# Attention stage: PSUM drained by ScalarE copies, the division moved to GpSimd, and TensorE's groups in a new order

## The chip, the cores and the metric

One NeuronCore of one Trainium2 chip runs the whole program. The metric is the device time of one execution in microseconds (us); lower is better. The engines are TensorE (PE; its weight loads are listed apart as PEld), VectorE (DVE), ScalarE (ACT), GpSimd (POOL) and SyncE (SP, which only starts transfers here).

## The reference, cut to what matters

Three parts follow one another: a linear attention over 4 batches of 576 tokens with 8 heads of 64, a soft mixture of 8 experts with 4 slots each, and a second mixture whose gate is balanced by eight Sinkhorn rounds. The change touches the attention and the slot statistics that run beside it.

```
proj = einsum('bhsd,df->bhsf', x, w_phi)            # for q and for k
proj = proj - max(abs(proj), axis=-1)
phi  = concatenate([exp(proj), exp(-proj)], -1)
kv   = einsum('bhsf,bhsd->bhfd', phi(k), v);  z = sum(phi(k), axis=s)
num  = einsum('bhsf,bhfd->bhsd', phi(q), kv)
den  = einsum('bhsf,bhf->bhs', phi(q), z) + 1e-06
x    = num / den                                     # then logits = x @ phi, softmax over tokens and over slots
```

## The kernel before

The 2304 tokens are 18 tiles of 128 (NT). One loop (line 449) drives the attention: step i works on the keys of tile i and, LAG = 7 steps behind, on the queries of tile t = i - 7. Steps 0 to 6 have keys only, steps 7 to 17 both, steps 18 to 25 queries only. All engines but GpSimd are wrapped in `InOrder` (line 441), so each of them executes in the order in which the code is written; GpSimd is wrapped only at line 527, after the attention.

The work of a step is made of groups; most of what they issue carries the helper's line L51 in the trace, so the tile's name tells the group:

- `project` (line 155; tiles pk, pq): 32 small matmuls into two PSUM banks, then on VectorE for each bank a maximum (mk, mq) and a subtraction (uk, uq), which empties the bank.
- `k_exp` (line 181): four exponentials on ScalarE from uk into phik.
- `kv_acc` (line 189): 64 matmuls of phik with the value tile vt into the accumulator kvacc, one for each batch that the tile touches. Tiles 4 and 13 touch two batches. `kv_finish` (line 208) copies the accumulator to kvs with three ScalarE copies. There is one accumulator buffer, tag "kv".
- `q_transpose` (line 228): 8 transposes of uq into two banks (ut), and behind each bank two ScalarE exponentials into phiq.
- `q_num` (line 255): for each half of the heads 32 matmuls into a bank (num); VectorE adds 1e-6 to the denominator column, takes the reciprocal (rd) and multiplies from PSUM into x.
- `x_turn` (line 281) turns x by 4 transposes (xt or, in the last steps, xl in the accumulator buffer), and ScalarE copies it to xT; `x_logits` (line 293) makes 16 matmuls (lg or xl), and ScalarE copies 32 columns.
- `slot_inputs` (line 306) is a generator. For every group g of four tiles (the last has two) it finds a running maximum (gmt, mx, al), spreads it (dg, gmb), takes exponentials (dd), counts (pcs) and sums x (psi, then si on VectorE); `slot_norm` (line 389) then normalises the logits, with a subtraction and a multiplication on GpSimd (L397, L404) and an exponential on ScalarE between them. The loop advances it by one piece at `si_step`.
- `load_v` (line 139) starts the transfer of a value tile and has GpSimd copy it into vt (L143) and set the ones (L147); vs and vt have two buffers each.

TensorE's order in a full step is: pq(t+1), pk(i+1), xt(t-1), ut(t), lg(t-1), kvacc(i), num(t). PSUM has five 512-column banks A to E beside the accumulator's three; `mm(name, bank)` takes a bank, and a new tile in a bank waits until all readers of the old one are done. In the query-only steps the order is pq(t+1), ut(t), xl(t-1), num(t), lg(t-1), with `halves` (line 223) choosing the banks so that ut and num have banks of their own.

After the last step the generator is run to its end: the last tile's turn and logits, the sums of group 3, the whole of group 4. Between these `keep_busy` (line 377) puts dummy transposes on TensorE. Then psit and sit give the slot inputs, and the first matmul of the expert stage (ph) starts.

The weights of the expert stages are loaded all along, by half units from ScalarE's queue (`load_half`) in steps 7 to 24 and by whole units from SP's (`load_units`); units 5, 6 and 10 wait for the buffers of the query pool (line 508).

Of the kernel before, what the change touches and what calls it, by code (L numbers as in the profile page):

```python
# [7 lines left out]
F32 = mybir.dt.float32  # L8
# [46 lines left out]
def tile_kernel(ctx: ExitStack, tc: tile.TileContext, a):  # L55
# [82 lines left out]

    def load_v(i):
        rows = kp.tile([128, DM], F32, tag="vs", name=f"vs{i}", bufs=2)  # L140
# [4 lines left out]
        parts = parts_of(t)  # L145
        for b1, r0, r1 in parts:
            G.memset(x[r0:r1, :, D:XW], float(b1 == b))  # L147
        vt_t[i] = x
# [6 lines left out]
    def project(pool, nm, x, t):  # L155

        pss, us = [mm(f"p{nm}{t}_{j}", ("AB" if nm == "q" or t < LAG and t % 2 else "CD")[j]) for j in range(2)], []
# [20 lines left out]
    def k_project(t):  # L178
        uk_t[t] = project(kp, "k", kt_t.pop(t), t)

    def k_exp(t):
        us = uk_t.pop(t)
        phik = kp.tile([128, H, 2, F], F32, tag="phik", name=f"phik{t}")
        for j in range(2):
            for c in range(2):
                A.activation(out=phik[:, j::2, c, :], in_=h4(us[j]), func=AF.Exp, scale=1.0 if c == 0 else -1.0)
        phik_t[t] = phik
# [29 lines left out]
    def q_project(t):  # L217
        uq_t[t] = project(qp, "q", qt_t.pop(t), t)

    def alone(i):  # L220
        return i + 1 >= NT

    def halves(t, hh, num=False):
        if t + LAG >= NT:
            return "DC"[hh] if num else "CE"[hh]
        return "EC"[hh] if alone(t + LAG) else "AE"[hh]

    def q_transpose(t, hh):
        ps = mm(f"ut{t}_{hh}", halves(t, hh))
        for j in range(4):  # L230
            PE.transpose(ps[:, j * 128:(j + 1) * 128], uq_t[t][hh][:, j * 128:(j + 1) * 128], ident)
        phiq_t[t, hh] = phiq = [qp.tile([128, 512], F32, tag="phiq", name=f"phiq{t}_{hh}_{c}", bufs=6) for c in range(2)]
        for c in range(2):
            A.activation(out=phiq[c], in_=ps, func=AF.Exp, scale=1.0 if c == 0 else -1.0)
        if hh:
            uq_t.pop(t)
# [7 lines left out]
    pair_t = {}  # L244

    def x_tile(t):
        n = (t + 2) % XR
        if n < 4:
            if n % 2 == 0 or t not in pair_t:
                pair = const.tile([128, 2, DM], F32, tag=f"xx{n // 2}", name=f"xx{t}", bufs=1)  # L250
                pair_t[t - n % 2], pair_t[t - n % 2 + 1] = pair[:, 0], pair[:, 1]
# [3 lines left out]
    def q_num(t, hh):  # L255
        if hh == 0:
            x_t[t] = x_tile(t)
        phiq = phiq_t.pop((t, hh))
        ps = mm(f"num{t}_{hh}", halves(t, hh, True))
        for c in range(2):  # L260
            for j in range(4):
                for g in range(2):
# [6 lines left out]
                    )  # L269
        pv = ps[:, 0:4 * XW].rearrange("p (h w) -> p h w", h=4)  # L270
# [7 lines left out]

    xT_t, xl_t = {}, {}

    def x_turn(t):
        if t + LAG + 1 >= NT:
            xl_t[t] = pacc.tile([128, 1536], F32, tag="kv", name=f"xl{t}")
            ps = xl_t[t][:, 0:512]
        else:
            ps = mm(f"xt{t}", "D" if alone(t + LAG + 1) else "E")
# [6 lines left out]
    def x_logits(t):  # L293
        xT = xT_t.pop(t)
        pl = xl_t.pop(t)[:, 512:1024] if t in xl_t else mm(f"lg{t}", "D" if alone(t + LAG + 1) else "B")
# [10 lines left out]
    def slot_inputs(g):  # L306

        ts, n = groups[g], len(groups[g])
        lgg = lg[:, ts[0]:ts[0] + n, :]
        gm4 = first.tile([128, 4, NS], F32, tag="gd", name=f"gm4{g}", bufs=1)  # L310
        if len(ts) == 2:
# [5 lines left out]
        yield  # L317
        last = g == len(groups) - 1
        pt = mm(f"gmt{g}", "B" if g > 1 else "C")
        keep_busy(last, 5)  # L320
        PE.transpose(pt[:, 0:128], gm4.rearrange("p g j -> p (g j)"), ident)
# [4 lines left out]
        dg = first.tile([NS, NS], F32, tag="gd", name=f"dg{g}", bufs=1)  # L326
        V.tensor_scalar_mul(dg, ident[0:NS, 0:NS], mx[0:NS])
        if g:
            al = first.tile([128, 1], F32, tag="al", name=f"al{g}", bufs=2)
# [3 lines left out]
        yield  # L333
        pm = mm(f"gmb{g}", "B" if g > 1 else "C")
        keep_busy(last, 6)
        PE.matmul(pm[:, 0:NS], ones[0:NS, :], dg, start=True, stop=True)
        dd = first.tile([128, 4, NS], F32, tag="gd", name=f"dd{g}", bufs=1)
        V.tensor_tensor(out=dd[:, 0:n], in0=lgg, in1=pm[:, 0:NS].unsqueeze(1).to_broadcast([128, n, NS]), op=ALU.subtract)
        A.activation(out=dd[:, 0:n], in_=dd[:, 0:n], func=AF.Exp)
        if last:  # L340

            V.tensor_scalar_mul(sels[32 * n:128], sels[32 * n:128], al[32 * n:128])
        yield
        ps, pc = mm(f"psi{g}", "A" if g else "B"), mm(f"pcs{g}", "B" if g else "C")
        keep_busy(last, 4)
        for i in range(n):
            PE.matmul(pc[32 * i:32 * i + 32, 0:2], dd[:, i], ones[:, 0:2], start=True, stop=True)
        for i in range(n):
            PE.matmul(ps[32 * i:32 * i + 32, :], dd[:, i], x_t.pop(ts[i]), start=True, stop=True)
        if g == 3:  # L350
            load_in_x(7)
        r = slice(0, 32 * n)
# [776 lines left out]
```

## Time and profile before

| | |
|---|---|
| median of 3 runs | 1007.1 us (1006.99 to 1008.5) |
| the profiled execution's own time | 1006.96 us |
| its span | 1005.2 us |
| busy share of the span | PE 99%, PEld 93%, DVE 70%, ACT 55%, POOL 57% |
| attention, up to the first ph matmul | 178.55 us from the span's start |
| granted TensorE clock | 1.00 (its upper level) in every stretch |

The span is what the trace covers; the execution's own time has 1.8 us more around it. Busy shares are averages over stages with different limits, and matmul records overlap, so a PE of 99% is not a PE at its peak. What a wait costs is read from the weight loads' idle time (PEld), from the chain of work that ended last and from the times at which groups start.

### The profile page before, as it was taken

To read this page: it belongs to the slowest core of one execution; us is meant where nothing else is said; L and a number is where in the kernel's file an instruction comes from. 1 tells how busy PE (TensorE), PEld (TensorE's weight loads), DVE (VectorE), ACT (ScalarE), POOL (GpSimd) and SP (SyncE) were. 2 spreads that over 40 slices of the span, in tenths; PEclk is the share of its full clock that TensorE was granted. 3 is DMA by queue.
4 is the path that set the end of the run, shared out by engine and by line. 5 is a ranking of instruction groups with operands and counts; after the bars stand their busy time and mean duration, and the time that the engine had idled before them with its cause. 6 is when DMAs were issued, how large, how long until landed. Compare 5 with 4: busy or idle time off the path is not lost.

```text
span 1005.2 us, 27875 instructions
## 1 busy us (share of the span) xinstructions
PE 991.4 (99%) x11638; PEld 936.8 (93%) x11638; DVE 698.9 (70%) x1414; ACT 552.8 (55%) x995; POOL 577.5 (57%) x438
## 2 busy tenths in 40 slices
PE   8999999999999999999999999999999999999998
PEld 7888887459999999999999999999999999999998
DVE  6777876367887676677667676676677667667665
ACT  5665654165666666655565556455555565465452
POOL 2101000135777677858785878578767867777543
PEclk9999999999999999999999999999999999999999
DMA  7766568991003100310031004000400130000111
GB/s 213 220 199 214 167 192 303 392 358 45 1 1 127 43 2 1 126 43 2 2 126 43 2 1 167 3 1 5 165 1 2 35 135 2 1 1 28 59 43 64
DMA packets 25485, 88.84 MB, mean 88 GB/s; under 512 B 3472, under 2 KB 6416, under 8 KB 19600
## 3 DMA queue, kind: packets, MB, share of 16 engines
q1 hardware_dynamic: 19984, 68.05, 19.2%
q10 hardware_dynamic: 5184, 18.88, 6.1%
q8 instruction: 92, 1.51, 0.6%
q14 instruction: 33, 0.27, 0.1%
q0 software_dynamic: 192, 0.13, 0.1%
HBM read 82.33 MB, written 4.72 MB: 87 GB/s over the span
## 4 chain that ended last, share of the span: by engine, by line
PE 96%; DVE 2%; issue 1%; ACT 1%; DVEq 0%; ACTq 0%
PE x L51 39%; PE y L51 20%; PE z L51 16%; PE kvacc L51 3%; PE num L51 3%; PE pq L51 2%; PE ut L51 2%; PE pk L51 2%; PE ps L51 2%; PE po L51 1%; PE ph L51 1%; PE lg L51 1%; PE xt L51 1%; PE xl L51 1%; PE psi L51 0%
## 5 line engine op out<-in xcount | busy, mean ns | idle before, releaser
L51 POOL TENSOR_TENSOR hl_s<-s,hh_s 128x512 fp32r<-128x512 f32 x286 | 365.5, 1300 | 208.2 <-ACT hh_s L51 189.8
L51 PE MATMUL x<-w_t,hh_s 128*128 128x256 f32 x1152 | 204.9, 278 | 0.1
L51 ACT ACTIVATE hh_s<-s 128x512 fp32r<-128x512 f32 x287 | 175.3, 630 | 51.1 <-DVE s L51 48.1
L51 ACT ACTIVATE r<-z 128x512 f32<-128x512 f32 x143 | 85.6, 598 | 166.0 <-PE z L51 164.9
L51 PEld LDWEIGHTS x<-w_t,hh_s 128*128 128x128 f32 x1152 | 173.4, 188 | 1.1 <-ACT xo L51 0.3
L51 DVE SCALAR_TENSOR_TENSOR xo<-x,P,xo 128x256 f32<-128x256 f32 x252 | 120.6, 479 | 70.2 <-PE x L51 70.2
L51 ACT ACTIVATE hh_a<-z 128x512 fp32r<-128x512 f32 x216 | 122.1, 600 | 73.0 <-DVE s L51 71.5
L51 PE MATMUL x<-w_t,hl_s 128*128 128x256 f32 x576 | 159.1, 277 | 0.0
L51 DVE SCALAR_TENSOR_TENSOR s<-z,r 128x512 f32<-128x512 f32 x143 | 98.0, 685 | 87.3 <-ACT hh_a L51 82.7
L51 DVE SCALAR_TENSOR_TENSOR hl_a<-z,hh_a 128x512 fp32r<-128x512 f32 x216 | 146.7, 679 | 2.7 <-ACT hh_a L51 2.7
L51 PEld LDWEIGHTS x<-w_t,hl_s 128*128 128x128 f32 x576 | 108.0, 188 | 0.0
L51 PE MATMUL y<-w_t,hh_s 128*128 128x256 f32 x576 | 103.0, 278 | 0.0
L51 PE MATMUL z<-w_b,hh_a 128*128 128x256 f32 x576 | 102.3, 278 | 0.0
L51 PE MATMUL y<-w_b,hh_s 128*128 128x256 f32 x576 | 101.7, 276 | 0.0
L51 PE MATMUL x<-w_t,hh_a 128*128 128x256 f32 x576 | 101.7, 276 | 0.0
L51 PE MATMUL x<-w_b,hh_a 128*128 128x256 f32 x576 | 101.4, 276 | 0.0
L51 DVE SCALAR_TENSOR_TENSOR s<-z,s 128x512 f32<-128x512 f32 x143 | 97.6, 682 | 3.5 <-POOL hl_s L51 1.4
L51 PEld LDWEIGHTS z<-w_b,hh_a 128*128 128x128 f32 x576 | 86.6, 188 | 2.9 <-issue 2.9
L51 PEld LDWEIGHTS y<-w_t,hh_s 128*128 128x128 f32 x576 | 87.4, 188 | 0.0
L51 PEld LDWEIGHTS y<-w_b,hh_s 128*128 128x128 f32 x576 | 86.8, 188 | 0.0
L51 PEld LDWEIGHTS x<-w_t,hh_a 128*128 128x128 f32 x576 | 86.8, 188 | 0.0
L51 PEld LDWEIGHTS x<-w_b,hh_a 128*128 128x128 f32 x576 | 86.6, 188 | 0.0
(188 smaller groups left out, 1977.1 us busy)
## 6 DMA issues: line engine op xcount, KB each, us to landing
moe_w<-in_moe_w SPq DMA_DIRECT2D x45, 1024.0 KB, 6.6
moe_w<-in_moe_w ACTq DMA_DIRECT2D x36, 512.0 KB, 4.2
vs<-in_vb SPq DMA_DIRECT2D x20, 256.0 KB, 4.1
kt<-in_kT SPq DMA_DIRECT2D x18, 256.0 KB, 3.7
qt<-in_qT SPq DMA_DIRECT2D x18, 256.0 KB, 3.5
out<-xo SPq DMA_DIRECT2D x18, 128.0 KB, 1.7
out<-xo SPq DMA_DIRECT2D x9, 256.0 KB, 2.0
moe_w<-in_moe_w SPq DMA_DIRECT2D x2, 512.0 KB, 10.2
```

The lines of the kernel that those rows point to most:

```text
L51: return lambda *args, **kwargs: self.tc.keep_in_program_order(make(*args, **kwargs))
```

## The change

The numerator no longer leaves PSUM through VectorE: two ScalarE copies per tile put num with its denominators into one SBUF tile, VectorE takes eight reciprocals at once, and GpSimd multiplies, in two instructions (`q_divide`); only the last tile keeps the old way. GpSimd now also runs in program order. `load_v` is split into the transfer and `place_v`, GpSimd's part, one step later. Turning and scoring of x(t-1) now come in the step of num(t), behind it. TensorE's order in a full step becomes num(t), xt(t-1), ut(t+1), pq(t+2), lg(t-1), kvacc(i), pk(i+1). The exponentials of the keys move to the start of their own step, between the copies of num. Each step names its five banks (n0, n1, k0, k1, q1) and rotates them; in the query-only steps they stay. The slot generator becomes plain calls placed by step number (`slot_early`, `slot_late`).

```diff
+    def place_v(i):
         x = kp.tile([128, H, XW], F32, tag="vt", name=f"vt{i}", bufs=2)
-        G.tensor_copy(out=x[:, :, 0:D], in_=rows.rearrange("p (h d) -> p h d", h=H))
+        G.tensor_copy(out=x[:, :, 0:D], in_=vs_t.pop(i).rearrange("p (h d) -> p h d", h=H))
...
-            u = pool.tile([128, 512], F32, tag=f"u{nm}", name=f"u{nm}{t}_{j}", bufs=2 if nm == "k" else 4)
+            u = pool.tile([128, 512], F32, tag=f"u{nm}", name=f"u{nm}{t}_{j}", bufs=2 if nm == "k" else 3)
...
+    def q_transpose(t, hh, bank):
+        ut_t[t, hh] = ps = mm(f"ut{t}_{hh}", bank)
...
+    def q_exp(t, hh):
+        ps = ut_t.pop((t, hh))
+        phiq_t[t, hh] = phiq = [qp.tile([128, 512], F32, tag="phiq", name=f"phiq{t}_{hh}_{c}", bufs=4) for c in range(2)]
         for c in range(2):
             A.activation(out=phiq[c], in_=ps, func=AF.Exp, scale=1.0 if c == 0 else -1.0)
...
-    XR = 7
+    XR = 8
...
+    def q_num(t, hh, bank):
         if hh == 0:
             x_t[t] = x_tile(t)
+            if t + 1 < NT:
+                den_t[t] = qp.tile([128, 2, 4, XW], F32, tag="num", name=f"nums{t}", bufs=1)
...
+        if t + 1 < NT:
+            A.copy(out=den_t[t][:, hh].rearrange("p j w -> p (j w)"), in_=ps[:, 0:4 * XW])
+            return
...
+    def q_divide(t):
+        nums = den_t.pop(t).rearrange("p h j w -> p (h j) w")
+        rd = qp.tile([128, 8, 1], F32, tag="rd8", name=f"rd{t}", bufs=2)
+        V.tensor_scalar_add(rd, nums[:, :, XW - 1:XW], 1e-6)
+        V.reciprocal(out=rd, in_=rd)
+        for hh in range(2):
+            G.tensor_tensor(
+                out=x_t[t].rearrange("p (h d) -> p h d", h=H)[:, hh::2, :],
+                in0=nums[:, 4 * hh:4 * hh + 4, 0:D], in1=rd[:, 4 * hh:4 * hh + 4].to_broadcast([128, 4, D]), op=ALU.mult,
+            )
...
-    PE, V, A, SP = (InOrder(tc, x) for x in (PE, V, A, SP))
+    PE, V, A, SP, G = (InOrder(tc, x) for x in (PE, V, A, SP, G))
...
+    n0, n1, k0, k1, q1 = "CDABE"
+    def slot_early(t, bank):
+        for g in range(LAST):
+            s = t - 4 * g
+            if s == 5:
+                slot_run(g, bank)
+            if s == 6:
+                slot_dd(g, bank)
+            if s == 7:
+                slot_sums(g, bank)
+                if g < 3:
+                    slot_norm(g, 0)
+            if s == 8 and g < 3:
+                slot_norm(g, 1)
+    def slot_late(t, bank):
+        for g in range(LAST):
+            if t - 4 * g == 4:
+                slot_max(g)
+            if t - 4 * g == 6:
+                slot_counts(g, bank)
-    for i in range(NT + LAG + 1):
+    for i in range(NT + LAG):
         t = i - LAG
+        for n in [n for n, (u, _) in enumerate(VBLOCKS) if u == i + 1]:
+            place_v(n)
...
+        if t + 2 < 0:
+            if len(bs) == 1:
+                k_project(i + 1, "CDAB"[(i + 1) % 2 * 2:][:2])
+            kv_acc(i, bs[0])
...
+            continue
+        q_only = i >= NT
+        if 0 <= t:
+            q_num(t, 0, n0)
+        if i in uk_t:
+            k_exp(i, 0, 0)
+        if 0 <= t:
+            q_num(t, 1, n1)
+        if 0 <= t - 1:
+            x_turn(t - 1, None if q_only else n0)
+        if i in uk_t:
+            k_exp(i, 0, 1)
+            k_exp(i, 1, 0)
+            k_exp(i, 1, 1)
...
+        if 0 <= t + 1 < NT:
+            q_transpose(t + 1, 0, n0 if q_only else k0)
+            q_transpose(t + 1, 1, n1)
+        if 0 <= t < NT - 1:
+            q_divide(t)
+        slot_early(t, q1)
+        if 0 <= t + 1 < NT:
+            q_exp(t + 1, 0)
+        if 0 <= t + 2 < NT:
+            q_project(t + 2, (k0, k1) if q_only else (k1, n0))
...
+        if 0 <= t - 1:
+            x_logits(t - 1, q1)
+        if 0 <= t + 1 < NT:
+            q_exp(t + 1, 1)
...
         if bs:
+            late = [(i - 1, b) for b, _, _ in parts_of(i - 1)[1:] if i - 1 >= LAG - 2]
+            for u, b in late + [(i, bs[0])]:
+                kv_acc(u, b)
...
+        slot_late(t, k1 if not q_only else q1)
         if i + 1 < NT:
+            k_project(i + 1, (k0, q1))
+            n0, n1, k0, k1, q1 = k1, n1, k0, q1, n0
+        elif i + 1 == NT:
+            n0, n1, k0, k1, q1 = k0, n1, k1, n0, q1
...
+    qstack.close()
...
+    load_units(wq, 5, 6, 10)
+    x_turn(NT - 1)
+    slot_dd(3, "B")
+    x_logits(NT - 1)
+    slot_max(4)
+    slot_counts(3, "C")
+    slot_sums(3, "A")
+    load_in_x(7)
+    slot_run(4, "B")
+    slot_dd(4, "C")
+    slot_counts(4, "D")
...
+    slot_sums(4, "A", count_all)
```

`slot_max`, `slot_run`, `slot_dd`, `slot_counts` and `slot_sums` are the pieces of `slot_inputs` in their old order and with their old instructions: maximum of the logits; gmt with mx, dg and al; gmb with dd; pcs with cs; psi with si. `slot_norm` is unchanged.

## Rows read from the trace of the kernel before

**Rows 1.** By stretch: length; PE, PEld, DVE, ACT, POOL busy; clock; DMA share, GB/s.
```profile
61.19:69.58 8.39, 8.21 (x221) 7.30 (x222) 6.77 (x15) 4.92 (x10) 0.67 (x2) 1.00 0.55 162
131.64:136.63 4.99, 4.98 (x126) 4.56 (x125) 4.53 (x13) 3.04 (x7) 0.55 (x2) 1.00 0.63 185
...
42.18:122.52 80.34, 78.75 (x2067) 69.03 (x2067) 65.22 (x145) 47.06 (x99) 7.50 (x24) 1.00 0.65 199
...
130.54:168.53 37.99, 36.57 (x844) 32.21 (x842) 29.58 (x84) 20.24 (x46) 2.18 (x6) 1.00 0.67 220
168.53:178.55 10.02, 9.18 (x103) 6.01 (x99) 5.71 (x23) 1.84 (x7) 2.02 (x4) 1.00 1.00 410
```

**Rows 2.** Waits of the weight loads from 36 to 124 us: total, times, longest.
```profile
PEld ut L51 <- PE xt L51: 3.0, 9, 0.3
PEld lg L51 <- DVE uq L51: 1.9, 9, 0.3
```

**Rows 3.** Timeline of the key-only steps: start, length, engine, line, operation.
```profile
14.12 2.21 PE L51 MATMUL kvacc<-vt,phik 128*64 128x65 f32 x64
...
16.25 0.86 PEld L51 LDWEIGHTS pk<-wbd,kt 64*64 64x64 f32 x32
...
16.46 0.61 POOL L143 COPY vt<-vs 128x512 f32<-128x512 f32 x1 [2.20 <-PE kvacc L51]
...
19.30 0.86 PEld L51 LDWEIGHTS pq<-wbd,qt 64*64 64x64 f32 x32
...
20.30 1.15 ACT L51 ACTIVATE phik<-uk 128x512 f32<-128x512 f32 x2 [0.18 <-DVE uk L51]
```

**Rows 4.** Groups by shape, 0 to 179 us: count, busy us, mean ns, idle before.
```profile
L51 ACT ACTIVATE phiq<-ut 128x512 f32<-128x512 f32 x72 | 37.2, 603 | 11.2 <-PE ut L51 10.2
...
L51 DVE TENSOR_TENSOR uq<-pq,mq 128x512 f32<-128x512 f32 x36 | 24.9, 691 | 1.2
...
L51 PEld LDWEIGHTS pk<-wbd,kt 64*64 64x64 f32 x576 | 17.0, 133 | 5.2 <-issue 3.2 <-DMA kt<-in_kT 1.5
...
L51 DVE TENSOR_TENSOR xx<-num,rd 128x256 f32<-128x256 f32 x20 | 8.5, 424 | 1.6 <-PE psi L51 0.9
...
L51 ACT COPY kvs<-kvacc 128x260 f32<-128x260 f32 x4 | 1.6, 395 | 0.0
```

**Rows 5.** Groups by shape on POOL, whole span; same columns.
```profile
L51 POOL TENSOR_TENSOR hl_s<-s,hh_s 128x512 fp32r<-128x512 f32 x286 | 365.5, 1300 | 208.2 <-ACT hh_s L51 189.8 <-DVE s L51 18.2
...
L397 POOL TENSOR_TENSOR lg<-lg,rm 128x128 f32<-128x128 f32 x3 | 1.2, 399 | 32.5 <-DVE rm L51 32.5
```

**Rows 6.** Timeline of one query-only step: start, length, engine, line, operation.
```profile
132.33 1.08 ACT L51 ACTIVATE phiq<-ut 128x512 f32<-128x512 f32 x2 [0.19 <-PE ut L51]
...
133.03 2.10 PE L51 MATMUL num<-kvs,phiq 128*64 128x65 f32 x64
...
134.96 0.62 PE L51 MATMUL xl<-phi,xT 128*64 128x32 f32 x16
...
135.51 1.10 PE L51 MATMUL pq<-wbd,qt 64*64 64x128 f32 x32
...
135.63 0.18 ACT L51 COPY lg<-xl 128x32 f32<-128x32 f32 x1 [0.76 <-PE xl L51]
```

**Rows 7.** Timeline of the slot chain and the end of the attention.
```profile
154.34 0.27 DVE L51 TENSOR_REDUCE rm<-lg 128x4 f32<-128x128 f32 x1
154.76 0.40 POOL L397 TENSOR_TENSOR lg<-lg,rm 128x128 f32<-128x128 f32 x1 [12.59 <-DVE rm L51]
...
170.56 1.04 PE L51 MATMUL psi<-xx,dd 128*32 128x512 f32 x8
...
...
171.70 0.75 DVE L51 SCALAR_TENSOR_TENSOR si<-si,al,psi 128x512 f32<-128x512 f32 x1 [0.63 <-PE psi L51]
...
172.90 0.30 PE L51 MATMUL gmt<-ident,gm 128*128 128x128 f32 x1
...
174.08 0.20 ACT L51 ACTIVATE al<-al 128x1 f32<-128x1 f32 x1 [1.66 <-DVE al L51]
```

More of the change, by code (lines that the diff above doesn't have):

```diff
@@ L153, in load_q, with project @@
         qt_t[t] = x
-    def project(pool, nm, x, t):
-        pss, us = [mm(f"p{nm}{t}_{j}", ("AB" if nm == "q" or t < LAG and t % 2 else "CD")[j]) for j in range(2)], []
+    def project(pool, nm, x, t, banks):
+        pss, us = [mm(f"p{nm}{t}_{j}", banks[j]) for j in range(2)], []
         for p in range(4):
@@ L176, in tile_kernel, with k_project, k_exp @@
     kvacc = {}
[L178 to L187, printed above, removed]
+    def k_project(t, banks):
+        uk_t[t] = project(kp, "k", kt_t.pop(t), t, banks)
+    def k_exp(t, j, c):
+        if (j, c) == (0, 0):
+            phik_t[t] = kp.tile([128, H, 2, F], F32, tag="phik", name=f"phik{t}")
+        A.activation(out=phik_t[t][:, j::2, c, :], in_=h4(uk_t[t][j]), func=AF.Exp, scale=1.0 if c == 0 else -1.0)
+        if (j, c) == (1, 1):
+            uk_t.pop(t)
     def kv_acc(t, b):
@@ L215, in kv_finish, with q_project @@
         kvs_t[b] = kvs.rearrange("p (j h c w) -> p j h c w", j=2, h=4, c=2)
[L217 to L229, printed above, removed]
+    def q_project(t, banks):
+        uq_t[t] = project(qp, "q", qt_t.pop(t), t, banks)
@@ L258, in q_num @@
         phiq = phiq_t.pop((t, hh))
-        ps = mm(f"num{t}_{hh}", halves(t, hh, True))
+        ps = mm(f"num{t}_{hh}", bank)
         for c in range(2):
@@ L285, in x_turn @@
         else:
-            ps = mm(f"xt{t}", "D" if alone(t + LAG + 1) else "E")
+            ps = mm(f"xt{t}", bank)
         for kc in range(KC):
@@ L343, in slot_inputs, with slot_dd @@
-        yield
-        ps, pc = mm(f"psi{g}", "A" if g else "B"), mm(f"pcs{g}", "B" if g else "C")
-        keep_busy(last, 4)
-        for i in range(n):
-            PE.matmul(pc[32 * i:32 * i + 32, 0:2], dd[:, i], ones[:, 0:2], start=True, stop=True)
+    def slot_dd(g, bank):
+        n = len(groups[g])
+        pm = mm(f"gmb{g}", bank)
+        keep_busy(g == LAST, 6)
+        PE.matmul(pm[:, 0:NS], ones[0:NS, :], run["dg"], start=True, stop=True)
+        dd_t[g] = dd = first.tile([128, 4, NS], F32, tag="gd", name=f"dd{g}", bufs=1)
+        V.tensor_tensor(out=dd[:, 0:n], in0=lgs(g), in1=pm[:, 0:NS].unsqueeze(1).to_broadcast([128, n, NS]), op=ALU.subtract)
+        A.activation(out=dd[:, 0:n], in_=dd[:, 0:n], func=AF.Exp)
+        if g == LAST:
+            V.tensor_scalar_mul(sels[32 * n:128], sels[32 * n:128], al_t[g][32 * n:128])
@@ new lines, in slot_counts, with slot_sums @@
+    def slot_counts(g, bank):
+        n = len(groups[g])
+        r = slice(0, 32 * n)
+        pc = mm(f"pcs{g}", bank)
+        keep_busy(g == LAST, 4)
+        for i in range(n):
+            PE.matmul(pc[32 * i:32 * i + 32, 0:2], dd_t[g][:, i], ones[:, 0:2], start=True, stop=True)
+        if g == 0:
+            V.tensor_copy(out=cs[r], in_=pc[r, 0:2])
+        else:
+            V.scalar_tensor_tensor(out=cs[r], in0=cs[r], scalar=al_t[g][r], in1=pc[r, 0:2], op0=ALU.mult, op1=ALU.add)
+    def slot_sums(g, bank, between=None):
+        ts, n = groups[g], len(groups[g])
+        r = slice(0, 32 * n)
+        dd = dd_t.pop(g)
+        ps = mm(f"psi{g}", bank)
@@ L454, in tile_kernel @@
             load_v(n)
[L455 removed]
+        for u in {2: [0], 4: [1], 5: [2]}.get(i, [t + 4] if 2 < t + 4 < NT else []):
             load_q(u)
```

187 lines of the change are left out of this document (65 added, 122 removed).

## The prediction, made before the change was run

> **What bounds the kernel now.** I read the page first: TensorE is busy through the span and keeps its upper clock, and the change ends where the expert stage begins, so only the attention's end can move. The stretches come next [rows 1]. A full step takes 8.39 us with 7.30 us of weight loads, a good query-only step 4.99 us. VectorE (6.77), ScalarE (4.92) and GpSimd (0.67) are below TensorE in a full step: TensorE sets the pace, and an engine relieved gains only what TensorE now waits for. The waits of the weight loads name that [rows 2]: in nine steps ut waits behind the turn of x, 0.3 us each, and lg for the bank that VectorE empties, 0.2 us each. Then the timelines of a key-only step, a query-only step and the end [rows 3, 6, 7].
>
> **The sum**, against the profiled execution's 1006.96 us, which lies 0.1 us under the median of 1007.1 us. Points in time are those of the trace; the expert stage's first matmul is at 178.55.
>
> Start (steps 0 to 7): more waits. Each projection keeps VectorE for four operations of some 0.69 us [rows 4], then come two pairs of exponentials of 1.15 us [rows 3]. Before, pk waits 3.2 us there [rows 4]. After, kv of tile 4 stands first in its step (pq(0) no longer covers it) and waits for exponentials that end at 21.45, 1.1 us after it could go on; pq(0) waits 0.65 us for pk(5)'s bank, ut(0) 1.5 us for pk(6)'s, pq(1) 0.5 us. These four are my count from the code with the durations just named; they make 3.75 us, so +0.5. By 42.18 [rows 1] the new order has also one pq and one ut more behind it, 1.9 us, so its step 8 starts at 44.6.
>
> Full steps: a gain. Nothing in the new order is asked for just when it is ready: the bank of x's turn comes free with the copy of num's first half 0.5 us ahead, lg has a pq between it and xT, pk finds its banks drained a group earlier. So a full step is the plain work of a query-only step (4.99) and of a key-only one, 19.30 - 16.25 = 3.05 [rows 1, 3]: 8.04. By weight loads, 4.56 and 2.81 of them against 7.30 seen in a step, it would be 7.97. I take 8.0; the ends are 8.39 (no gain) and 7.8. Nine such steps are 72.0 us. Step 17 has no pk: 7.0. The second batch of tile 13 is 1.9, psi 0.9 (the sum of group 1 has moved on to step 18), and the small groups of two slot chains 1.9, at 0.3 to 0.4 us each (gmt has 0.30 [rows 7]). Together 83.7 us.
>
> One wait in step 14, **the queue on GpSimd**. `place_v` for tile 15 needs the value buffer of tile 13's second batch, whose kv now runs in step 14 itself, behind lg. GpSimd is in order: its copy starts 0.13 us after that kv (before, 14.12 + 2.21 to 16.46) and takes 0.61 [rows 3]; behind it stand the two multiplies of `q_divide`, then the subtraction of `slot_norm`, 0.40 [rows 5], and ScalarE, in order too, has this norm's exponential ahead of those of ut. pk(15) wants ut's bank. A multiply of 128x256 has no row: 0.40 us for 128 columns and 1.30 for 512 [rows 5] bound it, and on the line between it is 0.69, which I take. From kv's end 0.13 + 0.61 + 1.38 + 0.4 + 0.3 + 1.08 of exponentials [rows 6], with some 0.15 of hand-overs, is 4.0; the other kv, 2.0, fills half of it. So 2.0 us of wait (1.4 to 3.2 with the bounds).
>
> VectorE's multiply from PSUM takes 0.424 us [rows 4]. The Trainium skill's GPSIMD Engine Reference (Performance versus the Vector engine) says that GpSimd is the wrong place for elementwise arithmetic with two inputs, measured there at 1.96 times VectorE. By that it would be 0.83 us, an estimate, and the wait 0.3 us longer.
>
> So step 18 starts at 44.6 + 83.7 + 2.0 = 130.3. In rows 1 its counterpart is 130.54.
>
> Query-only steps: **two banks for four tiles**. In these steps num's first half, ut's first half and the next num share n0, the second halves n1. num's second half must wait for both exponentials of ut's second bank, and ScalarE has the copy of lg ahead of them, which waits for lg, TensorE's last group of the step. The chain from lg's end: 0.05 to the copy, some 0.07 until the next can start, 1.08 for two exponentials, 0.1 back to TensorE: 1.3 [rows 6]. In its shadow lies num's first half, half of 134.96 - 133.03, so 0.93 after its start. Each step waits 0.37: 5.35 instead of 4.98. Where a slot piece puts something before the first exponentials, more. psi to si 1.14, si 0.75 [rows 7], rm and the way to GpSimd 0.42 and the subtraction 0.40 [rows 7], the norm's exponential and 1.08: some 4.1 us from ut's end, under which TensorE has psi, pq (1.10) and lg (0.55) [rows 6], 2.5 in all; that is a wait of 1.6, and 0.3 more at the second half. This hits steps 18 and 22 (t = 11, 15). At t = 13 the exponential al comes 1.18 us after gmt [rows 7] and costs 0.7. From step 18's start to the end of num(17): 9.6 (both nums), 5.35, 6.0, 5.6, 7.7 and 4.25 (no pq): 38.5. So num(17) ends at 168.8; before, at 168.53 [rows 1].
>
> End: the new order has turn and logits of tile 16 behind num(17), and one accumulator buffer, so the last turn waits for lg(16)'s copy instead of x(17): turn of 16, copy, lg and copy make 2.2 us behind num(17), the division of x(17) 1.4 (my estimates from the durations above). psi of group 3 (1.04 [rows 7]) now stands between the last logits and gmt instead of under the copy of xT. +0.8 and +1.0, -0.1 for shorter VectorE queues: 11.7 instead of 10.02 [rows 1].
>
> The sum: 168.8 + 11.7 = 180.5, which is 1.95 after 178.55. 1006.96 + 1.95 gives **1008.9 us**, 1.8 over the median.
>
> Costed at nothing: the 34 copies of num on ScalarE (0.395 us for this shape [rows 4]) and the multiplies elsewhere. A full step's ScalarE then has 4.92 + 0.8 of 8.0 us, and x is wanted a whole step later. Uncovered, the copies would cost 0.4 a half. VectorE loses two multiplies a tile, 0.85 us [rows 4], which gives nothing by itself. The loads of units 5, 6 and 10 still follow num(17); DMA is full from there, with a share of 1.00 [rows 1], and as ph comes later behind num(17) their cover grows. SP's value loads wait for `place_v` but are two steps early.
>
> **Rivals.**
> - Faster: the exponentials of ut are not held up by the norm. If the subtraction gets through GpSimd and VectorE before lg ends, step 14 loses its 2.0 and steps 18 and 22 lose 1.5 each: 1008.9 - 5.0 = 1003.9, and the gain of the full steps, 9 x 0.39 = 3.5, shows. For it: GpSimd starts its subtraction 0.42 us after rm does [rows 7], so the norm itself is short. Against: rm stands behind si, and si behind psi, on an in-order queue. It decides where the norm's exponential ends less than 1.3 us after ut.
> - Slower: ScalarE is the bound of the tail. If its operations don't overlap (exponentials 0.6 each, the copy of lg 0.2 whole), the chain of each query-only step grows by 0.15 for every operation in it, the steps to 5.45, those with slot pieces by 0.4 more, together 2.0: 1010.9. For it: one exponential is 0.603 [rows 4], so the 1.08 for two [rows 6] rests on an overlap. Against: ScalarE has 3.04 of 4.99 us there. It decides from the point where ScalarE is still at work when num's first half ends.
> - The full step does not shrink: ut or lg finds another wait of the size of rows 2, and 3.5 us are not gained: 1012.4.
>
> **How the numbers follow.** A measurement of this kernel tells about 0.2%, 2 us, from no change. The forecast lies just under that. My case has 0.42, the faster rival 0.28, the two slower ones 0.22 and 0.08. My own case spreads by the bounds of the multiply (-0.6 to +1.2) and of the full step (-1.8 to +3.5), so a third of it lies beyond +2. That gives faster 0.26, same 0.36, slower 0.38. The range for 8 in 10 reaches from just under the faster rival, 1003.5, to between the slower ones, 1011.5; the likeliest case alone has 1007 to 1010.5.
>
> **What would show it.** Full steps of 8.0 us with no wait of ut and lg; one hole of 2 us before pk in step 14, released by ScalarE, with GpSimd's copy of vt in the middle of the step; query-only steps of 5.3 to 5.4 us where num waits for ScalarE's phiq; two holes near 1.6 us behind psi; 11.7 us from num(17) to ph. Query-only steps of 5.0 us, or no hole in step 14, would make it wrong on the fast side; full steps of 8.4 us on the slow side.

## The result, and the profile after

The change makes the kernel slower: 1015.45 us (1011.89 to 1016.9, five runs) against 1007.1 us (1006.8 to 1008.5, five runs), a ratio of 1.0073 (95%: 1.0051 to 1.0094). A second series of the same two kernels (e5 below) gave 1014.2 against 1007.86 us, 1.0066 (1.0053 to 1.0078). Forecast were 1008.9 us and a range of 1003.5 to 1011.5. The profiled execution took 1015.84 us with a span of 1014.1, 8.9 more than before.

The forecast had given points in time, so the miss can be located:

| point | forecast | after | added to the miss |
|---|---|---|---|
| num of step 8 starts | 44.6 | 46.22 | 1.6 |
| num of step 18 starts | 130.3 | 134.92 | 3.0 |
| num of the last block ends | 168.8 | 174.03 | 0.6 |
| ph, the expert stage, starts | 180.5 | 186.46 | 0.7 |
| from there to the end | 826.7 | 827.6 | 1.0 |

The busy times by stretch in the kernel after (same columns as [rows 1]); in this order a full step, step 8, step 14, step 20 of the query-only ones, all of those, and the end:

```profile
65.04:73.07 8.03, 8.03 (x222) 7.38 (x224) 5.36 (x10) 5.45 (x12) 1.85 (x4) 1.00 0.62 194
46.22:56.55 10.33, 8.29 (x224) 7.50 (x220) 5.72 (x10) 6.48 (x15) 1.84 (x4) 1.00 0.63 199
98.50:111.26 12.76, 11.03 (x294) 9.47 (x293) 5.91 (x11) 5.75 (x13) 2.76 (x7) 1.00 0.48 154
147.42:153.92 6.50, 5.51 (x134) 4.85 (x130) 5.03 (x13) 3.63 (x11) 1.47 (x3) 1.00 0.63 200
134.92:174.03 39.11, 35.37 (x812) 30.33 (x805) 22.42 (x55) 22.61 (x55) 9.19 (x18) 1.00 0.63 197
174.03:186.46 12.43, 9.97 (x103) 6.60 (x103) 5.88 (x24) 2.51 (x8) 2.31 (x5) 1.00 1.00 403
```

A full step takes 8.03 us instead of 8.39 [rows 1] and TensorE is busy in all of it: the gain is there. VectorE falls from 6.77 to 5.36 us a step, ScalarE rises from 4.92 to 5.45 and GpSimd from 0.67 to 1.85. Step 8 has TensorE idle for 2.0 of 10.33 us, step 14 for 1.7 of 12.76, the query-only steps for 3.7 of 39.11.

The waits of the weight loads from 36 to 135 us (total, times, longest); those of ut for xt [rows 2] are gone, those of lg for VectorE are down from nine to two of 0.2 us (eight more of up to 0.2 us stand under "issue"; the matmuls in front cover them, since TensorE is busy in all of a full step), and two long ones have come:

```profile
PEld num L51 <- issue: 3.9, 11, 2.2
PEld pk L51 <- ACT phiq L51: 1.9, 1, 1.9
```

The second is the wait forecast for step 14. Its timeline is as forecast, with GpSimd's copy in the middle:

```profile
106.64 0.61 POOL L51 COPY vt<-vs 128x512 f32<-128x512 f32 x1 [8.21 <-PE kvacc L51]
107.25 1.19 POOL L51 TENSOR_TENSOR xx<-nums,rd 128x256 f32<-128x256 f32 x2
108.39 0.40 POOL L51 TENSOR_TENSOR lg<-lg,rm 128x128 f32<-128x128 f32 x1
108.83 0.31 ACT L51 ACTIVATE lg<-lg 128x128 f32<-128x128 f32 x1 [5.41 <-POOL lg L51]
109.05 1.06 ACT L51 ACTIVATE phiq<-ut 128x512 f32<-128x512 f32 x2
110.16 1.17 PE L51 MATMUL pk<-wbd,kt 64*64 64x128 f32 x32 [1.73 <-ACT phiq L51]
```

The first was not forecast. Step 8's timeline shows TensorE stopping inside one group, after 54 of the 64 matmuls of num; the profile names no releaser, and from 49.2 us on VectorE, ScalarE and GpSimd are idle too:

```profile
46.22 1.85 PE L51 MATMUL num<-kvs,phiq 128*64 128x65 f32 x54
50.10 0.51 PE L51 MATMUL num<-kvs,phiq 128*64 128x65 f32 x10 [2.04 <-issue]
```

One row of the DMA queues, from 47.50 to 47.75 us (packets, MB, share of 16 engines), led to a theory. A block of 16 KB of instructions begins to arrive there, at 47.56; the block before had begun at 39.85, while in undisturbed steps they come 4 to 5 us apart:

```profile
q8 instruction: 1, 0.02, 24.6%
```

ScalarE's queue had started two halves of expert weights, 512 KB each, shortly before. In the kernel before, the same two halves started 2.8 us apart, at 37.85 and 40.69; in the new order they start 0.65 us apart. The next half, that of step 8, starts only behind the hole, so the 1 MB of step 7 alone can bear on it. The DMA engines were 84 to 93% busy from 42 to 46 us. In the timeline of after:

```profile
42.01 0.38 ACTq L51 DMA_DIRECT2D moe_w<-in_moe_w  x1
42.66 0.34 ACTq L51 DMA_DIRECT2D moe_w<-in_moe_w  x1
51.25 0.33 ACTq L51 DMA_DIRECT2D moe_w<-in_moe_w  x1
```

TensorE, then, may have had no instructions left. The Trainium skill (Runtime: NRT & Kernel Launch, Instruction fetch mechanics) says that an engine's instructions are streamed in 16 KiB blocks by a DMA queue of its sequencer, at a cost that is mostly hidden. The size agrees with this row; whether the cost is hidden is what the runs ask.

### The profile page after: what moved, and what is told of

It reads as the page before. It is cut to its first block, busy times and chain, and to the rows that moved or that the text cites. A ratio compares the mean times of both kernels' runs of the same rounds, so it can differ in the third digit from the quotient of the medians.

```text
span 1014.1 us, 27882 instructions
## 1 busy us (share of the span) xinstructions
PE 992.6 (98%) x11638; PEld 939.3 (93%) x11638; DVE 682.1 (67%) x1344; ACT 563.0 (56%) x1029; POOL 597.2 (59%) x472
## 4 chain that ended last, share of the span: by engine, by line
PE 94%; DMA 2%; ACT 1%; DVE 1%; issue 1%; POOL 0%; ACTq 0%; DVEq 0%
PE x L51 39%; PE y L51 19%; PE z L51 16%; PE num L51 4%; PE kvacc L51 3%; PE pk L51 2%; DMA moe_w<-in_moe_w 2%; PE pq L51 2%; PE ps L51 1%; PE po L51 1%; PE ut L51 1%; PE ph L51 1%; PE xl L51 1%; PE lg L51 1%; PE xt L51 1%
```

## The experiments

All runs in one table. Times in us of the profiled execution; "query-only" is from num of step 18 to num of the last block, "end" from that num's end to ph. Each ratio is against runs of the kernel before in the same series; their medians were 1007.1 us for after, 1009.17 for e1 to e4, 1007.86 for e5 to e8 and 1010.01 for e9 to e11.

| run | num of step 8 | step 8 | step 14 | query-only | end | ph | ratio to before (95%) |
|---|---|---|---|---|---|---|---|
| after | 46.22 | 10.33 | 12.76 | 36.89 | 12.4 | 186.46 | 1.0073 (1.0051 to 1.0094) |
| e5, after again | 46.29 | 9.45 | 12.76 | 36.89 | 12.4 | 184.72 | 1.0066 (1.0053 to 1.0078) |
| e1, norm late | 45.54 | 9.23 | 10.89 | 36.23 | 12.4 | 182.09 | 1.0017 (0.9998 to 1.0036) |
| e2, three vt | 46.24 | 9.24 | 10.89 | 36.87 | 12.4 | 183.05 | 1.0036 (1.0019 to 1.0054) |
| e3, weights later | 46.17 | 8.03 | 12.75 | 36.88 | 12.4 | 184.80 | 1.0051 (1.0035 to 1.0068) |
| e4, VectorE divides | 47.78 | 9.86 | 13.51 | 39.01 | 13.7 | 205.28 | 1.0250 (1.0220 to 1.0281) |
| e6, scores first | 46.01 | 9.77 | 10.89 | 32.02 | 12.4 | 179.06 | 1.0002 (0.9992 to 1.0012) |
| e7, end regrouped | 47.64 | 14.44 | 12.76 | 36.90 | 11.3 | 190.06 | 1.0076 (1.0060 to 1.0091) |
| e8, all mended | 45.50 | 8.03 | 10.89 | 32.02 | 12.9 | 178.44 | 0.9985 (0.9969 to 1.0001) |
| e9, turns back | 45.39 | 8.02 | 10.89 | 32.02 | 11.3 | 176.49 | 0.9958 (0.9944 to 0.9972) |
| e10, start banks | 43.90 | 8.03 | 10.89 | 32.01 | 10.7 | 175.16 | 0.9960 (0.9945 to 0.9976) |
| e11, weights back | 44.04 | 10.48 | 10.89 | 32.02 | 10.7 | 175.74 | 0.9977 (0.9963 to 0.9992) |

The expert stage behind ph is the same program in all of them and took 825.6 to 830.7 us in these executions, so ph is the sharper measure of an edit, the ratio that of the kernel.

**The norm in step 14 (e1, e2).** e1 moves its first half behind the step's kv; e2 gives vt a third buffer:

```
# e1, in slot_early: taken out; in slot_late: put in
+            if t - 4 * g == 7 and g < 3:
+                slot_norm(g, 0)
# e2
-        x = kp.tile([128, H, XW], F32, tag="vt", name=f"vt{i}", bufs=2)
+        x = kp.tile([128, H, XW], F32, tag="vt", name=f"vt{i}", bufs=3)
```

> The first half of the slot norm (VectorE's maxima, GpSimd's subtraction, ScalarE's exponential) is moved from the middle of its step to behind the step's accumulation of keys and values; nothing else moves. Theory A (the norm's exponential stands in ScalarE's queue ahead of the exponentials of ut and waits there for a GpSimd that is itself held, by the copy of vt in step 14 and by its multiplies in steps 18 and 22): step 14, from the start of num to the start of the next num, falls from 12.76 us to 8.0 to 8.5, steps 18 and 22 fall from 7.40 and 7.64 to about 6.0 each; 4.4 + 1.4 + 1.6 = 7.4 us less than the changed kernel, about 1008. Rival B (what is late in these steps is GpSimd's result x or the copy of vt itself, and TensorE would only wait one group later, in the turn of x or in the accumulation of the next step): the three steps and the one after each lose less than 1.5 us together, and the time stays above 1013.5.

> The placed values get three buffers instead of two, so that GpSimd's copy in step 14 need not wait until the late accumulation of step 13's block has read its buffer; the norm stays where it is. Theory A (GpSimd's queue is held by that copy): the copy runs some 8 us earlier, the multiplies wait for the copies of num alone, and step 14 falls from 12.76 us to between 8.0 and 9.2; steps 18 and 22 stay at 7.4 and 7.6, since there is no copy of vt in them; 3.6 to 4.7 us less than the changed kernel, about 1011. Rival B (the two multiplies of 0.6 us and the norm's subtraction hold ScalarE whatever the copy does, as in steps 18 and 22): step 14 keeps a wait of 1.3 us or more and stands at 9.5 or above, 3 us less at the most. Rival E (the wait is not of GpSimd at all): 12.8 as before.

Step 14 went from 12.76 to 10.89 in both, and the wait of pk is gone from both. The 8.0 to 8.5 and 8.0 to 9.2 written down were a slip: the forecast itself has the second batch of tile 13 and psi in this step, some 2.9 us more than a full step. The wait was 1.87 us, and either half of its cause removed is enough: in e2 the norm still stands ahead of the exponentials, but its exponential starts 6.0 us after the step's num instead of 10.3, with GpSimd's multiplies long done, and pk waits for nothing:

```profile
102.97 0.31 ACT L51 ACTIVATE lg<-lg 128x128 f32<-128x128 f32 x1 [1.08 <-POOL lg L51]
106.82 1.10 PE L51 MATMUL pk<-wbd,kt 64*64 64x128 f32 x32
```

In the query-only steps rival B was right about e1: step 18 fell from 7.40 to 6.00 us, but step 19 rose from 5.1 to 6.23. The norm's exponential then stood ahead of the next step's copies of num, and ut waited for those:

```profile
140.26 0.31 ACT L51 ACTIVATE lg<-lg 128x128 f32<-128x128 f32 x1 [1.67 <-POOL lg L51]
140.74 0.38 ACT L51 COPY nums<-num 128x260 f32<-128x260 f32 x1
140.89 0.88 PE L51 MATMUL ut<-ident,uq 128*128 128x128 f32 x6 [0.50 <-ACT nums L51]
```

**The hole in step 8 (e3, e5, e11).** e3 moves the loads of two weight units out of steps 7 and 8 into steps 16 and 17 (the first halves are shown; the second ones move in the same way):

```
-    attn_units = {7 + n: (wa, n) for n in range(4)}
+    attn_units = {7 + n: (wa, n) for n in range(2, 4)}
+    twice = {16: (wa, 0), 17: (wa, 1)}
...
+        if i in twice:
+            load_half(*twice[i], 0)
```

> The expert weights that ScalarE's queue fetches in steps 7 and 8 (two units, 2 MB) are fetched in steps 16 and 17 instead; the instructions and their order on TensorE, VectorE and GpSimd are the same. In the changed kernel TensorE stands 2.04 us in the middle of num in step 8 with no operand missing, and the fetch of a block of instructions that begins at 47.5 us, as the weights' packets end, comes 2.4 to 2.6 us before it goes on. Theory C (TensorE has run out of instructions, whose fetch came late behind the weights' packets): with no weights in steps 7 and 8 the next block's fetch begins 4 to 5 us after the one before it and not 7.75 us, the hole is gone or under 0.4 us, step 8 takes 8.0 to 8.5 instead of 10.33, and the time is about 2 us less than the changed kernel's, 1013.5, unless a hole opens in steps 16 and 17. Rival D (the hole belongs to the place in the program, or to a wait that the profile does not name): it stays between the same instructions with 1.5 us or more, and the time is within 0.7 us.

> The changed kernel once more, on the same chip as the three below. Theory C (TensorE now and then runs out of instructions, whose blocks are fetched late behind other transfers, so the hole varies from execution to execution): the hole inside num of step 8 has another length than 2.04 us (the two kernels with the same program up to there showed 0.94 us, at the same instruction), other steps show holes of up to 0.6 us that the first profile did not have, and the time is 4 to 9 us above the kernel before on the same chip. Rival D (a fixed wait of the program): 2.04 us again, within 0.1.

In e3 num runs through, and the block that had come at 47.56 us came at 44.11. The timeline of e3:

```profile
46.17 2.09 PE L51 MATMUL num<-kvs,phiq 128*64 128x65 f32 x64
48.19 0.66 PE L51 MATMUL xt<-ident,x 128*128 128x128 f32 x4
```

Step 8 took 8.03 us. Smaller holes opened elsewhere (0.49 us in step 9, 0.52 us where the weights had gone), so that ph came 1.7 us earlier and not 2.3. In e5, the same kernel as the one forecast, the hole was 0.94 us, before the same ten records, so it is no fixed wait; the new holes in other steps that theory C had also expected of e5 did not come. e11 is e10 with the weights back in steps 7 and 8:

> The same kernel as the start_banks run, but with the weights of two units fetched in steps 7 and 8 again, as in the changed kernel. Theory C (the fetch of TensorE's instructions is late behind the weights' packets): step 8 shows a hole of 0.9 to 3.7 us again, inside num, where the kernel without these weights has none, and the time is 0.5 to 2 us more. Rival D: no hole of more than 0.4 us, the same time within 0.5 us.

The hole came back, in e11's timeline:

```profile
48.07 0.51 PE L51 MATMUL num<-kvs,phiq 128*64 128x65 f32 x10 [2.19 <-issue]
```

ph came only 0.6 us later than in e10, which has holes of 0.45, 0.69 and 0.46 us in steps 9, 13 and 17 instead.

Over all profiles: in the seven with weights in steps 7 and 8 and the new order on TensorE (after, e1, e2, e5, e6, e7, e11) the block came 5.8 to 10.1 us after the one before, and the hole was 2.04, 0.94, 0.94, 0.94, 1.47, 3.69 and 2.19 us, always before the same ten records. TensorE went on 1.2 to 1.6 us after the block's packet had ended, whether the packet came late or took long (in e5 it came early and took 2.2 us, in the others 1.0). In the four without (e3, e8, e9, e10) the block came 4.3 to 4.6 us after the one before, with no hole in step 8. In e4 the block came 7.2 us after the one before, but TensorE, slower there, needed it only 1.9 us after its packet's end. That it is the weights, by their times those of step 7, is shown; whether two halves 2.8 us apart, as before, would have left a hole was not run.

That TensorE lacks instructions can be read from the traces, though no row names a releaser. Number TensorE's records from 0 in the order of their start, semaphore instructions included. The gap of step 8 stands before record 2241 = 193 + 8 x 256 in all seven profiles. In the thirteen traces TensorE has 27 gaps of 0.2 us or more inside a group for which no releaser is named, and all of them stand before a record whose number is 193 plus a multiple of 256. The queue q8 brings 92 blocks to TensorE's 23,575 records in after, which is one for every 256 records; and record 193 + 256 m never starts sooner than 1.19 us after the end of the queue's m-th packet, in any of the thirteen traces. So TensorE stands until its next block is there, and a late block shows as a gap if TensorE gets to the border first. The weights are only one cause of a late block: the holes of steps 9, 13 and 17 lie at such borders too. The Trainium skill's "mostly hidden" holds at most of these borders, and does not hold at these 27.

**Is the division needed for the order? (e4)** The new order with the division of before on VectorE:

```
-        if 0 <= t < NT - 1:
-            q_divide(t)
...
-        if t + 1 < NT:
-            A.copy(out=den_t[t][:, hh].rearrange("p j w -> p (j w)"), in_=ps[:, 0:4 * XW])
+        if False:
+            A.copy(out=den_t[t][:, hh].rearrange("p j w -> p (j w)"), in_=ps[:, 0:4 * XW])
```

> The new order of the groups with the division of before: num is read from PSUM by VectorE (sum, reciprocal, multiply for each half), the ScalarE copies and the GpSimd multiplies are left out. Theory F (the new order needs num's bank free at once, since the turn of x writes it two groups later): VectorE comes to the first half only behind the four operations on the keys' projection, 2.8 us after the step's start, and needs 0.8 us more, so that the turn of x starts at 3.6 instead of 2.2 us; full steps take 9.2 to 9.7 instead of 8.0, and ten of them make 12 to 15 us more, less some 3 us of the wait in step 14, for which GpSimd no longer has multiplies ahead of the norm: 1021 to 1028. Rival G (VectorE has room, being busy 5.6 to 7.2 of 8.0 us in a step, and the order alone brings the shorter step): full steps of 8.0 to 8.4, and the time is within 3 us of the changed kernel or below it.

Theory F, and worse than it expected: full steps of 9.85 us, ph 18.8 us later, and 1035.9 us in all instead of 1021 to 1028, though VectorE is busy only 6.69 us of a step. The row to read is xt's wait for VectorE, which reaches num only behind the keys' four operations:

```profile
70.39 0.15 DVE L51 TENSOR_SCALAR rd<-num 128x4 f32<-128x4 f32 x1
71.36 0.63 PE L51 MATMUL xt<-ident,x 128*128 128x128 f32 x4 [1.78 <-DVE rd L51]
```

So with VectorE's operations in this order the new order on TensorE needs the copies on ScalarE to run at 8.03 us. Two things were not run: an order in which VectorE takes num ahead of the keys' operations, and the new division in the old order.

**The query-only steps (e6).** ScalarE's exponentials of ut come first, lg's matmuls and copy behind them, and the norm's subtraction runs on VectorE, ahead of the sums:

```
-        slot_early(t, q1)
         if 0 <= t + 1 < NT:
             q_exp(t + 1, 0)
+        slot_early(t, q1)
...
-        if 0 <= t - 1:
+        if 0 <= t - 1 and not q_only:
             x_logits(t - 1, q1)
         if 0 <= t + 1 < NT:
             q_exp(t + 1, 1)
+        if 0 <= t - 1 and q_only:
+            x_logits(t - 1, q1)
...
+                if g < 3:
+                    slot_norm(g, 0)
                 slot_sums(g, bank)
-                if g < 3:
-                    slot_norm(g, 0)
...
-            W.tensor_tensor(out=cc, in0=cc, in1=rm.to_broadcast([128, n, NS]), op=ALU.subtract)
+            V.tensor_tensor(out=cc, in0=cc, in1=rm.to_broadcast([128, n, NS]), op=ALU.subtract)
```

> On ScalarE the exponentials of ut go ahead of what can wait: the first half's ahead of the slot operations, in the query-only steps the second half's ahead of the copy of lg; the norm's subtraction runs on VectorE instead of GpSimd, ahead of the sums of the slots. Theory A (in steps 14, 18 and 22 the exponentials wait for a norm held by GpSimd; in the other query-only steps they lose 0.3 us to the copy of lg, and 0.7 us in step 21 to the running maximum's exponential): step 14 falls from 12.76 to 10.9, and the six query-only steps from 36.9 us to 32.5 to 34 in all; 4.8 to 6.3 us less at the point where the experts' stage begins. Rival H (these steps are bound by the sum of TensorE's and ScalarE's work, and what is taken out of the way of the exponentials comes back as a wait for num's copies or for lg, as when the norm was moved to the step's end: 36.2 instead of 36.9): query-only steps 36 or more.

Theory A: 36.89 became 32.02 us, a little more than expected. By step: 18 lost 1.40, 20 lost 1.39 (the expectation calls it 21; the exponential al stands ahead there), 22 lost 1.65, and the other three 0.13 to 0.15 each. Three steps of e6 (19, 20, 22) show TensorE without a gap, so nothing more is to be had there from ScalarE. What each of these edits is worth alone was not run. The stretches of the three steps:

```profile
138.48:143.46 4.98, 4.98 (x131) 4.57 (x128) 3.97 (x10) 3.18 (x8) 1.54 (x3) 1.00 0.70 234
143.46:148.54 5.08, 5.08 (x131) 4.67 (x129) 4.17 (x12) 3.03 (x9) 1.48 (x3) 1.00 0.62 209
154.14:160.13 5.99, 5.99 (x141) 4.74 (x134) 4.51 (x11) 3.62 (x9) 1.23 (x2) 1.00 0.59 185
```

**The end (e7, e8, e9).** In the kernel after, one short wait follows another behind the last num:

```profile
175.35 0.66 PE L51 MATMUL xl<-phi,xT 128*64 128x32 f32 x16 [0.62 <-ACT xT L51]
176.29 0.66 PE L51 MATMUL xl<-ident,x 128*128 128x128 f32 x4 [0.29 <-ACT lg L51]
177.68 0.66 PE L51 MATMUL xl<-phi,xT 128*64 128x32 f32 x16 [0.40 <-ACT xT L51]
179.56 0.29 DVE L51 TENSOR_TENSOR gm<-lg 128x128 f32<-128x128 f32 x1 [1.95 <-PE psi L51]
```

e7 turns the last x into a bank of its own and reorders what follows:

```
+        if t == NT - 1:
+            x_turn(t, "C")
         if 0 <= t - 1:
             x_logits(t - 1, q1)
...
-    x_turn(NT - 1)
     slot_dd(3, "B")
-    x_logits(NT - 1)
-    slot_max(4)
+    x_logits(NT - 1, "E")
     slot_counts(3, "C")
+    slot_max(4)
+    slot_run(4, "B")
     slot_sums(3, "A")
...
-        keep_busy(g == LAST, 5)
```

> Only the order behind num of the last step differs: the last x is turned into a bank of its own instead of waiting for the copy of lg of the x before it, lg of the last x follows at once, the maximum of the last two blocks goes to TensorE ahead of the sums of the four before (its tiles have buffers of their own, so that it need not wait until those sums are read), and five turns that only fill TensorE's time are left out. Theory I (the end is 2.4 us longer than before because these waits follow one another: 0.62, 0.29 and 0.40 us for xT and lg, 1.0 us of VectorE for the sums, 0.6 us of filling): from the end of num of the last block to the experts' stage 10.0 to 10.6 us instead of 12.4. Rival J (the end is one chain of short operations of VectorE and ScalarE, which these waits only fill): 11.7 or more.

The end took 11.3 us: 1.1 gained, half of what theory I expects and more than J allows. Its total was lost elsewhere, by a longer hole and by the granted clock (PEclk, the last but two of the columns). The clock was at its lower level from 34.6 to 38.0 us, behind the wait of 1.62 us before ut, which left it at 1.00 in nine other profiles; num of step 8 started 1.4 us later for it, at 47.64. Then the hole of step 8 was 3.69 us long in this execution, and the clock fell again, so that step 8 took 14.44 us, 6.4 more than 8.03:

```profile
34.59:38.00 3.41, 3.36 (x54) 3.04 (x56) 1.09 (x3) 3.08 (x6) 0.00 (x0) 0.50 0.27 76
53.00:58.00 5.00, 4.82 (x46) 4.36 (x49) 0.38 (x2) 3.30 (x7) 1.19 (x2) 0.50 0.35 109
```

e8 has the edits of e2, e3, e6 and e7 together, and pq(0) back in step 4:

> The changed kernel with all of it: the queries' first projection back in step 4, three buffers for the placed values, the weights of steps 7 and 8 fetched in steps 16 and 17, the exponentials of ut first and the norm's subtraction on VectorE, the end regrouped. If the theories hold, the experts' stage begins 1.5 (start) + 1 to 2 (the hole of step 8) + 1.9 (step 14) + 3 (query-only steps) + 2 (end) = 9.4 to 10.4 us earlier than at 186.46 us, at 176 to 177 us against 178.55 in the kernel before, and the time is 1.5 to 2.5 us under the kernel before on the same chip. Rival (the holes open at other places, or the start is bound by VectorE's two projections whatever their order): 179 us or later, and the time is within 2 us above the kernel before.

The time is 2.0 us under the kernel before, as expected, but the interval of the ratio reaches 1.0001. ph, at 178.44, lies between theory and rival. It misses 176 to 177: the start gave 0.7 instead of 1.5, small holes opened in steps 9, 13, 15 and 17, and the end grew to 12.9 us. In this end the clock fell, and psi took 1.94 us instead of 1.04 [rows 7]; the stretch and the row in e8's timeline:

```profile
169.70:173.40 3.70, 3.62 (x16) 1.50 (x16) 1.49 (x5) 0.20 (x1) 0.00 (x0) 0.54 1.00 379
```

```profile
170.10 1.94 PE L51 MATMUL psi<-xx,dd 128*32 128x512 f32 x8
```

e7's profile shows the same end without the turns at a clock of 1.00, so the fall does not follow from the order of the end alone. e9 is e8 with the five turns back in slot_run:

```
+        keep_busy(g == LAST, 5)
         PE.transpose(pt[:, 0:128], gm_t.pop(g).rearrange("p g j -> p (g j)"), ident)
```

> The kernel with everything mended, with the five turns put back that only fill TensorE's time while VectorE takes the maximum of the last two blocks. In the kernel without them the granted clock was 0.54 of the upper level from 169.7 to 173.4 us, and the sums of the slots took 1.94 us instead of 1.04, the next six filling turns 1.49 instead of 0.88. Theory K (that idleness let the clock fall to the lower level): the turns, 0.77 us, stand in a wait of 0.70 us, the clock stays at 1.00, the sums take 1.04 us again, and the experts' stage begins 1.2 to 1.6 us earlier than without them, seen from the end of num of the last block (12.8 us there): 11.2 to 11.6. Rival L (the clock falls there anyway, for what came before): 12.8 to 13.5.

Theory K: psi took 1.06 us, the end 11.3, and the kernel is faster than before, by 0.4%. It does not rest on one profile: the mean clock of an execution was under 1.00 in ten of e8's eleven and in one of e9's nine. The timeline of e9:

```profile
168.70 0.77 PE L51 MATMUL busy<-ident 128*128 128x128 f32 x5
169.64 1.06 PE L51 MATMUL psi<-xx,dd 128*32 128x512 f32 x8
```

**The start (e10).** On top of e8:

```
-            k_project(i + 1, (k0, q1))
+            k_project(i + 1, (q1, k0) if t == -2 else (k0, q1))
...
-            q_transpose(t + 1, 0, n0 if q_only else k0)
+            q_transpose(t + 1, 0, n0 if q_only else q1 if t == -1 else k0)
...
-    slot_run(4, "B")
-    slot_sums(3, "A")
+    slot_sums(3, "A", lambda: slot_run(4, "B"))
```

> The kernel with everything mended, with two further edits. First, the keys' projection of step 6 is written into banks E and A instead of A and E, and the first half of the first ut into C instead of A, so that it need not wait until VectorE has read the keys' projection there (a wait of 1.62 us at 32.6 us that the profile calls issue). Theory M (that wait is the bank): ut follows the projection within 0.1 us, and num of step 8 starts 0.8 to 1.3 us earlier, at 44.2 to 44.7 us. Rival N (VectorE's queue, with three projections of 2.77 us in a row, is the bound of steps 5 to 7): ut is early, but what follows waits, and step 8 starts within 0.3 us of 45.5. Second, at the end the maximum of the last two blocks goes behind the sums of the slots on TensorE and no turns only fill the time there: with the clock kept, the end takes 10.6 to 11.2 us from the last num instead of 12.8. Both: the experts' stage begins at 175.2 to 176.5 us and the time is 2.5 to 4 us under the kernel before.

Theory M, and more than the 0.8 to 1.3 us it expected: num of step 8 starts 1.6 us earlier than in e8. What the profile of after calls "issue" was a bank still to be read by VectorE: ut starts 0.1 us after the subtraction that reads the bank ends, and this gap stands before a group and at no border of a block. First the rows of after, then that of e10:

```profile
32.44 0.69 DVE L51 TENSOR_TENSOR uk<-pk,mk 128x512 f32<-128x512 f32 x1
33.23 1.06 PE L51 MATMUL ut<-ident,uq 128*128 128x128 f32 x8 [1.62 <-issue]
```

```profile
30.44 1.09 PE L51 MATMUL ut<-ident,uq 128*128 128x128 f32 x8
```

Step 8 starts at 43.90, and ph comes at 175.16, 3.4 us before that of the kernel before. The time, 0.9960, is not under e9's: the expert stage took 830.1 us in e10's profile and 826.1 in e9's. Some 0.8 us of the difference come up 24 to 56 us behind ph, where po waits for VectorE's hz in e10 (0.72 us) and not in e9, and 3.0 us between 125 and 260 us, where one matmul of x takes 281 ns on average instead of 277, at a granted clock of 1.00 in both. Why stays open. e10's end, 10.7 us as expected, has no filling turns, and its clock was 1.00 in all six executions: the turns matter in e8's order, not in every one.

## Why the prediction was wrong

- **Full steps, 8.0 us**: right, 8.03; TensorE is busy in all of such a step, as its row in the table by stretch shows.
- **"Together 83.7 us" for steps 8 to 17**: the step that failed. It took these steps to be the plain work of their groups and nothing else, and so put at nothing that TensorE can stand still for want of instructions. With step 14's wait it was 85.7 us; 88.70 were measured. The late blocks cost 2.3 us in step 8 (by step length, against 8.03), 0.4 in step 9 and 0.8 in step 13; without them it would have been 85.2. How much it is differs between executions: in e5's the same steps took 86.9 us, 1.2 over the forecast, and there the start, 1.7 us, is the largest part of the miss. The sign was to be had. In the kernel before, too, a pk stops after eight records, at a border of a block; this wait is part of the 3.2 us that [rows 4] give for pk, which the forecast took for waits for VectorE:

```profile
36.34 0.89 PE L51 MATMUL pk<-wbd,kt 64*64 64x128 f32 x24 [1.23 <-issue]
```

- **The wait in step 14**: right in mechanism and size, 1.87 us against 2.0. The multiply of 128x256 took 0.61 us (mean of 34), against 0.69 from the line (0.70 by its own two ends). By the Trainium skill's GPSIMD Engine Reference (Performance versus the Vector engine) it would have been 0.83, an estimate; next to VectorE's 0.424 [rows 4] the 0.61 is 1.4 times, not the 1.96 measured there for 2048 elements.
- **Query-only steps**: right in kind, 39.1 against 38.5 us, but the sum is nearer than its terms, which is partly luck. By what e6 took away, the norm's waits cost 1.40 and 1.65 (forecast 1.6 + 0.3 each); al cost 1.39, not 0.7; the bank chain 0.15 a step, not 0.37 (half of 134.96 - 133.03 is 0.97, so its own rows give 0.33).
- **Start, "step 8 starts at 44.6"**: mis-sized by 1.6 us. The bank waits were there as counted (ut(0) 1.62 for 1.5), but the exponentials that kv of tile 4 waits for ended at 22.30 instead of 21.45, 0.85 late: 0.3 from the first loads on, the rest from a hole in pk(4), which took 1.77 us instead of 1.10. The hole lies at a border of a block, the term that steps 8 to 17 lack too; in e5 there is none, and all of the delay, 0.9 us, is there before pk(4). The pq of step 6 took 1.37 us instead of 1.1, in e1 to e6 too, so that is no late block; some 0.4 us more have no name here. e10 shows that 1.6 us of such a start lie in two choices of banks.
- **End, 11.7**: 12.4. The sequence was right. The 0.7 us more lie somewhere in the chain of short operations and the filling turns; no run tells which, and e7 and e10 show only that 1.1 and 1.7 us can be had there by another order.
- **The rest of the span** was taken as unchanged; it took 1.0 us more, within what it varies by.
- **Rivals**: the faster one needed the norm off the exponentials' way. It did not happen, but e6 makes it happen: step 14 and the query-only steps give 1.87 + 4.87 = 6.7 us, more than the 5.0 it was given, mainly since al's 1.4 was not in it.

So the direction and the named waits held, and the size fell short mainly because the sum knew only waits between the program's own instructions.

## What to carry to other kernels

Where a new order removes every small wait, look at what else an in-order engine can stand for. An "issue" gap inside one group, with the other engines idle, was a lack of instructions here; one before a group was a bank whose reader the profile does not name. The DMA view, the place of the gap among the engine's records and an exchange of banks told the two apart. Look also at when a new order starts its background loads: here it brought two halves of weights together that had been 2.8 us apart. On an in-order queue put what the critical engine waits for ahead of side work that depends on a third engine: the edits of e6 were together worth 0.6% here, as much as the whole change had lost. Work that only fills an engine's time is taken out only with an eye on the granted clock.

## What was not expected of the hardware

- A gap of TensorE varies from execution to execution of the same TensorE instructions (0.94 to 3.69 us at one place in seven profiles), with 1 MB of weights in flight, and is absent in four profiles without them.
- TensorE's gaps without a releaser inside a group (27 of 0.2 us or more in thirteen traces) all stand 256 records or a multiple of it apart, and it went on 1.2 us or more after the end of a 16 KB packet of its instruction queue.
- A long gap costs twice: in e7, with 3.69 us of idleness in step 8, the granted clock was 0.50, the lower of the two levels, from 53 to 58 us, and the step lost 2.7 us beyond the gap.
- At the end of the attention the same kind of order kept a clock of 1.00 in one kernel (e7) and had 0.54 for 3.7 us in another (e8); five turns of 0.77 us in all brought it back (e9), and so did another order without them (e10).
